# A Fourier filter ahead of a mixture of experts: dense transform replaced by a two-stage transform of 48 by 52 points

## Chip, cores, metric

One core of one Trainium2 chip. The metric is the device time of one execution in microseconds (us), the median of repeated runs.

## The reference

Each of 8 sequences of 2496 tokens and 256 channels is filtered along the tokens in the Fourier domain. Each token then goes to the best of 8 experts.

```python
X = np.fft.rfft(x, axis=1)                       # x: (8, 2496, 256) f32
F = (filt_r + 1j * filt_i)[None, :, :]           # (1249, 256)
y = np.fft.irfft(X * F, n=x.shape[1], axis=1)
# ... x = y.reshape(19968, 256)
logits = x @ w_gate + modality_bias[modality_id]
e_idx = np.argmax(logits, axis=1)                # top 1
# ... per expert e, on its tokens:
h = np.maximum(x[mask] @ w1[e], 0.0)
out[mask] = gate_w[mask, None] * (h @ w2[e])
```

## The kernel before

The filter is a dense transform: cosine and sine tables of 2496 by 1249 are generated on the chip, forward and inverse are plain matmuls in 16 bit. The output goes to DRAM as `xm_d`. Everything behind it (gating, sort, scatter, experts, gather) reads `xm_d` and is not changed. (The name `BF16` in the code stands for float16.)

```python
for cg in range(n_cg):                     # 4 groups of 512 columns (2 sequences)
    # ... x[b, s0:s0+sw, :] loaded in 128 KB pieces, cast to f16 on VectorE
    for kt in range(n_kt):
        ps_r = fpp.tile([P, CG], F32, tag="psr")
        ps_i = fpp.tile([P, CG], F32, tag="psi")
        for st in range(n_st):
            nc.tensor.matmul(ps_r[:kw, :], lhsT=fcos[:sw, st, k0:k0 + kw], rhs=xr[:sw, st, :], ...)
            nc.tensor.matmul(ps_i[:kw, :], lhsT=fmsin[:sw, st, k0:k0 + kw], rhs=xr[:sw, st, :], ...)
        # ... four products with the filter on VectorE, sum and difference on GpSimd
        # ... stored to Yr_d, Yi_d
# ... inverse tables generated
for cg in range(n_cg):
    # ... Yr_d, Yi_d loaded
    for nt in range(n_st):
        ps = ipp.tile([P, CG], F32, tag="ips")
        for kt in range(n_kt):
            nc.tensor.matmul(ps[:nw, :], lhsT=icos[:kw, kt, n0:n0 + nw], rhs=yrs[:kw, kt, :], ...)
            nc.tensor.matmul(ps[:nw, :], lhsT=imsin[:kw, kt, n0:n0 + nw], rhs=yis[:kw, kt, :], ...)
        # ... copied on ScalarE, stored to xm_d
# ...
xTc = gwp.tile([P, N], BF16, name=f"xTall{dc}")
nc.sync.dma_start_transpose(xTc, xm_d[:, dc * P:(dc + 1) * P])   # first reader of all of xm_d
```

## Time and profile before

| | us |
|---|---|
| median of 3 runs | 2477.0 |
| span of the profiled run | 2468.9 |
| filter (until the first transposing read of `xm_d`) | 1063.6 |
| all the rest | 1405.3 |

The first transposing read of `xm_d` cannot begin before the last store of the filter has landed, and nothing of the rest can begin before it. So its start splits the time in two, in both kernels. I call it the filter's end. The lines are in the prediction.

### The profile page before, as it was taken

The page shows a single profiled execution, that of the slowest core. Times are in us where ns is not written, and L with a number is a line of the kernel's source. Part 1 is how long each engine was busy: PE and PEld are TensorE (multiplying, and loading weights), DVE is VectorE, ACT ScalarE, POOL GpSimd, SP SyncE. Part 2 cuts the span into 40 slices and gives each one's busy share as a digit, 9 for nine tenths or more (in the row PEclk, how much of TensorE's full clock was granted, in tenths as well). Part 3 has the DMA queues.
Part 4 walks back from the last instruction along what each step waited for, and adds up shares of the span by engine and source line. Part 5 has one row for each costly group of instructions (what it writes and reads, how often), then busy time and mean ns, then how long its engine had stood idle before and what let it go on. Part 6 is the DMA issues. An engine that isn't in the chain of part 4 may idle for free. (4 is left out here: it accounts for less than half of the span.)

```text
span 2468.9 us, 22991 instructions
## 1 busy us (share of the span) xinstructions
PE 1283.3 (52%) x7228; PEld 617.4 (25%) x7228; DVE 634.8 (26%) x1325; ACT 443.8 (18%) x775; POOL 445.6 (18%) x487
## 2 busy tenths in 40 slices
PE   2469786876339999912000000000899999991000
PEld 0014232322114444402000000000555555550000
DVE  6873233323770000007100000000233333332122
ACT  4320000000341111101000000000455555550000
POOL 0012222221000000000013333345000000006665
PEclk9999898978669999965555555555999999996555
DMA  2112222211101221190971111117222222224466
GB/s 73 37 49 66 64 61 64 63 45 63 41 6 39 69 71 29 32 172 4 37 230 53 52 53 53 51 43 224 77 75 76 76 72 76 76 67 145 138 185 204
DMA packets 319271, 192.16 MB, mean 78 GB/s; under 512 B 172580, under 2 KB 306678, under 8 KB 319158
## 3 DMA queue, kind: packets, MB, share of 16 engines
q1 hardware_dynamic: 306678, 160.01, 25.8%
q0 software_dynamic: 12480, 30.69, 4.4%
q8 instruction: 65, 1.06, 0.2%
q14 instruction: 48, 0.39, 0.1%
HBM read 80.93 MB, written 87.38 MB: 68 GB/s over the span
## 5 line engine op out<-in xcount | busy, mean ns | idle before, releaser
L487 PE MATMUL hps<-w1sb,xT 128*128 x736 | 249.1, 380 | 555.5 <-DMA xT<-xs_d 555.5
L498 DVE COPY hT_sb<-hTps 128x512 f16<-128x512 f16 x368 | 156.3, 425 | 885.5 <-PE hTps L497 885.5
L182 PE MATMUL ps_i<-xr,fmsin 128*128 128x512 f16 (+2 forms) x800 | 325.9, 420 | 89.3 <-ACT fmsin L121 88.6
L238 PE MATMUL ps<-yrs,icos 128*128 128x512 f16 (+2 forms) x800 | 315.7, 395 | 103.6 <-ACT icos L125 83.3
L180 PE MATMUL ps_r<-xr,fcos 128*128 128x512 f16 (+2 forms) x800 | 324.2, 418 | 81.4 <-DVE xr L170 64.4
L491 ACT ACTIVATE h_sb<-hps 128x512 f16<-128x512 f32 x368 | 220.8, 600 | 625.8 <-PE hps L487 610.1
L240 PE MATMUL ps<-yis,imsin 128*128 128x512 f16 (+2 forms) x800 | 314.3, 393 | 0.0
L517 POOL DMA_INDIRECT ot<-os_d,pos_i32c x156 | 148.2, 950 | 572.2 <-DVE pos_i32c L514 502.9
L501 PE MATMUL ops<-w2sb,hT_sb 128*128 x1472 | 240.3, 272 | 0.3 <-DVE hT_sb L498 0.2
L487 PEld LDWEIGHTS <-xT 128*128 128x128 f16 x736 | 64.2, 98 | 570.5 <-issue 557.5
L449 POOL DMA_INDIRECT xs_d<-xg,pos_i x156 | 148.8, 954 | 267.8 <-DMA xs_d<-xg,pos_i 238.2
L501 PEld LDWEIGHTS <-hT_sb 128*128 128x128 f16 x1472 | 134.9, 97 | 67.6 <-DVE hT_sb L498 46.1
L182 PEld LDWEIGHTS <-fmsin 128*128 128x128 f16 (+2 forms) x800 | 83.2, 106 | 271.2 <-ACT fmsin L121 105.8
L497 PE MATMUL hTps<-ident,h_sb 128*128 128x128 f16 x1472 | 144.1, 220 | 13.1 <-ACT h_sb L491 0.5
L202 POOL TENSOR_TENSOR yr<-t,t 128x512 f16<-128x512 f32 (+1 forms) x40 | 50.9, 1272 | 487.6 <-DVE t L199 268.6
L238 PEld LDWEIGHTS <-icos 128*128 128x128 f16 (+2 forms) x800 | 80.8, 101 | 211.9 <-ACT icos L125 109.0
L497 PEld LDWEIGHTS <-h_sb 128*128 128x128 f16 x1472 | 97.4, 97 | 131.8 <-ACT h_sb L491 103.8
L180 PEld LDWEIGHTS <-fcos 128*128 128x128 f16 (+2 forms) x800 | 83.0, 106 | 155.1 <-issue 46.8
L121 ACT ACTIVATE imsin<-fr,zbias 128x1280 f16<-128x1280 f32 (+3 forms) x20 | 26.7, 1335 | 502.6 <-DMA yis<-Yi_d 442.9
L170 DVE CAST xr<-tmp 128x256 f16<-128x256 f32 (+1 forms) x160 | 50.1, 313 | 232.7 <-DMA tmp<-in_x_dram 232.7
L240 PEld LDWEIGHTS <-imsin 128*128 128x128 f16 (+2 forms) x800 | 81.1, 101 | 99.1 <-issue 12.2
L506 ACT COPY osb<-ops 128x256 f32<-128x256 f32 x184 | 68.4, 372 | 206.9 <-PE ops L501 205.1
(108 smaller groups left out, 737.5 us busy)
## 6 DMA issues: line engine op xcount, KB each, us to landing
os_d<-osb SPq DMA_DIRECT2D x184, 128.0 KB
out_dram<-ot SPq DMA_DIRECT2D x156, 128.0 KB
tmp<-in_x_dram SPq DMA_DIRECT2D x152, 128.0 KB
xs_d<-zz SPq DMA_DIRECT2D x23, 512.0 KB
xg<-xm_d SPq DMA_DIRECT2D x156, 64.0 KB
xm_d<-yo SPq DMA_DIRECT2D x152, 64.0 KB
tmp<-in_moe_w_dram SPq DMA_DIRECT2D x16, 512.0 KB
tmp<-in_moe_w_dram SPq DMA_DIRECT2D x64, 128.0 KB
```

The lines of the kernel that those rows point to most:

```text
L180: nc.tensor.matmul(ps_r[:kw, :], lhsT=fcos[:sw, st, k0:k0 + kw], rhs=xr[:sw, st, :], start=(st == 0), stop=(st == n_st - 1))
L182: nc.tensor.matmul(ps_i[:kw, :], lhsT=fmsin[:sw, st, k0:k0 + kw], rhs=xr[:sw, st, :], start=(st == 0), stop=(st == n_st - 1))
L238: nc.tensor.matmul(ps[:nw, :], lhsT=icos[:kw, kt, n0:n0 + nw], rhs=yrs[:kw, kt, :], start=(kt == 0), stop=False)
L240: nc.tensor.matmul(ps[:nw, :], lhsT=imsin[:kw, kt, n0:n0 + nw], rhs=yis[:kw, kt, :], start=False, stop=(kt == n_kt - 1))
L449: nc.gpsimd.indirect_dma_start(out=xs_d[:, :], out_offset=IOA(ap=pos_i32[:, t:t + 1], axis=0), in_=xg[:, :], in_offset=None)
L487: nc.tensor.matmul(hps, lhsT=xTs[dc][:, nsl], rhs=w1sb[:, ds(ej, 1), dc, fc * 512:(fc + 1) * 512], start=(dc == 0), stop=(dc == n_dc - 1))
L491: nc.scalar.activation(h_sb[:, fc * 512:(fc + 1) * 512], hps, AF.Relu)
L497: nc.tensor.transpose(hTps[:, k, :], h_sb[:, ft * P:(ft + 1) * P], ident)
L498: nc.vector.tensor_copy(hT_sb[:, fg * 4:(fg + 1) * 4, :], hTps)
L501: nc.tensor.matmul(ops, lhsT=hT_sb[:, ft, :], rhs=w2sb[:, ds(ej, 1), ft, :], start=(ft == 0), stop=(ft == n_ft - 1))
L506: nc.scalar.copy(osb, ops)
L517: nc.gpsimd.indirect_dma_start(out=ot[:, :], out_offset=None, in_=os_d[:, :], in_offset=IOA(ap=pos_i32c[:, t:t + 1], axis=0))
```

## The change

The intent: 2496 = 48 x 52, so the transform can be done as 48-point transforms (stage 1), twiddles and 52-point transforms (stage 2), the product with the filter, 52-point inverse (still stage 2), and 48-point inverse (stage 3). This takes 496 matmuls of 512 columns where there were 3200. The matrices are small and made on the chip. Between the stages, rows and columns swap through DRAM (`b1_d`, `b2_d`). The experts are untouched. The diff, cut to the new stages:

```diff
-    # dense tables, forward and inverse loops (see above)
+    N1, N2 = 48, 52                       # NS = 24, NTT = 26, KA = 96, KB = 104
+    # ... w1m, wbm (96 x 96), w2m, a1m, a2m (24 matrices of 104 x 104) made from iota and Sin
+    gen = tc.alloc_tile_pool(name="gen", bufs=1)          # their scratch
+    # ...
+    for src, dst in ((w2m, a1m), (w2x, a2m)):
+        for s0 in range(0, NS, SPB):
+            # ... 8 transposes on TensorE into tp
+            nc.vector.tensor_copy(
+                dst[:, s0:s0 + SPB, :].rearrange("p s (jr t) -> p s t jr", jr=4),
+                tp[:, :, :KB].rearrange("p s (t jr) -> p s t jr", jr=4))
+    gen.release()
+    # ... filter loads, 18 DMAs on GpSimd (f32 to f16)
+    with tc.tile_pool(name="fx", bufs=3) as xp, tc.tile_pool(name="fr", bufs=3) as rp, \
+         tc.tile_pool(name="fbig", bufs=2) as bp, tc.tile_pool(name="fpsum", bufs=4, space=PSUM) as pp:
+        def stage1(g):
+            # ... x of two half groups: nc.gpsimd.dma_start(xt[:, bi, :, :], xb[:, t0:t1, :])
+            for t in range(0, NTT, EV):                    # EV = 2: 1024 columns
+                # ... 2 matmuls with w1m into ps
+                t1_sb = rp.tile([KA, EV, CG], BF16, tag="t1")
+                nc.scalar.copy(t1_sb, ps[:KA])             # every sixth on VectorE
+                nc.sync.dma_start(b1_d[g, t:t + EV].rearrange("t p c -> p t c"), t1_sb)
+        def stage2(g):
+            for hh in range(NH):                           # 2 halves of 6 pairs
+                # ... t2: 4 loads from b1_d on SyncE
+                for s in range(0, sn, EV):
+                    # ... 2 forward matmuls: ps <- w2m, t2
+                    nc.scalar.copy(xf, ps[:KB])
+                    nc.vector.tensor_mul(p1, xf, g1[...])
+                    nc.vector.tensor_mul(p2, xf, g2[...])
+                    pz = pp.tile([P, EV, CG], F32, tag="ps")
+                    # ... 4 inverse matmuls: pz <- a1m, p1 and a2m, p2
+                    nc.scalar.copy(z, pz[:KB])
+                    nc.sync.dma_start(b2_d[g, ...], z)
+        def stage3(g):
+            for hh in range(NH):
+                # ... t4: 4 loads from b2_d on SyncE
+                for t in range(0, tn, EV):
+                    # ... 2 matmuls with wbm into ps
+                    nc.vector.tensor_scalar_mul(yo[...], ps[...], 1.0 / S)
+                for bi in range(BPG):
+                    nc.sync.dma_start(xm_d[...], yo[:, bi, :, :])
+        for g in range(NG + 2):                            # NG = 4
+            if g < NG: stage1(g)
+            if 0 < g <= NG: stage2(g - 1)
+            if g > 1: stage3(g - 2)
```

## The prediction

> **What bounds the kernel now.** I read the busy digits first, then a table of stretches cut where the work changes, then the groups by shape. The program is a chain of stages, and no engine bounds all of it, so each stage has to be read by itself.
>
> ```profile
> PE   2469786876339999912000000000899999991000
> PEclk9999898978669999965555555555999999996555
> DMA  2112222211101221190971111117222222224466
> ```
>
> The filter fills slices 1 to 17; the rest is gating, sorting, scatter, experts and gather. The stretches:
>
> ```profile
> core 0: us, PE busy (x) PEld busy (x) DVE busy (x) ACT busy (x) POOL busy (x), PEclk, DMA share, GB/s
> 0.00:597.00 597.00, 417.93 (x1600) 161.84 (x1600) 254.16 (x431) 63.95 (x62) 104.33 (x90) 0.93 0.19 56
> 597.00:736.00 139.00, 43.69 (x113) 14.71 (x114) 104.72 (x98) 51.36 (x39) 0.00 (x0) 0.61 0.12 38
> 736.00:1064.00 328.00, 324.52 (x1491) 146.06 (x1488) 4.32 (x8) 48.38 (x81) 0.14 (x1) 0.99 0.16 48
> 1064.00:1113.00 49.00, 0.93 (x29) 0.88 (x30) 3.16 (x3) 0.25 (x2) 0.00 (x0) 0.50 1.30 212
> 1113.00:1178.00 65.00, 13.30 (x321) 12.30 (x317) 45.93 (x215) 9.48 (x40) 1.23 (x2) 0.50 0.00 1
> 1178.00:1271.00 93.00, 0.59 (x2) 0.50 (x2) 8.72 (x46) 0.00 (x0) 2.57 (x3) 0.50 1.33 159
> 1271.00:1663.00 392.00, 0.00 (x0) 0.00 (x0) 0.00 (x0) 0.00 (x0) 149.35 (x157) 0.50 0.17 51
> 1663.00:1722.00 59.00, 0.00 (x0) 0.00 (x0) 0.00 (x0) 0.00 (x0) 35.05 (x69) 0.50 0.73 229
> ...
> 2229.00:2469.00 240.00, 1.44 (x12) 0.83 (x12) 57.95 (x158) 0.37 (x1) 148.23 (x156) 0.51 0.57 172
> ```
>
> Three rows are the filter: forward transform (597 us, 1600 matmuls, PE 70% busy, stalls while cosine tables are generated and x arrives in 128 KB pieces), inverse tables (139 us, DVE 75% busy), inverse transform (328 us, PE 99% busy). So 1064 us of 2469 are PE and table work for a dense 2496-point transform. From 1064 on, everything waits for the complete filtered tensor: two transposing DMA reads start at 1063.6 us. The remaining 2468.9 - 1063.6 = 1405 us are untouched by the change, and they cannot start early in either version. The 8.1 us between the span and the median of 2477.0 I carry over too.
>
> The durations that I need for the new stages:
>
> ```profile
> L238 PE MATMUL ps<-yrs,icos 128*128 128x512 f16 x684 | 270.0, 395 | 95.0 <-ACT icos L125 74.7 <-DMA yis<-Yi_d 20.4
> L506 ACT COPY osb<-ops 128x256 f32<-128x256 f32 x184 | 68.4, 372 | 206.9 <-PE ops L501 205.1 <-issue 1.8
> L243 ACT CAST yo<-ps 128x512 f16<-128x512 f32 x76 | 44.2, 585 | 261.2 <-PE ps L240 248.7 <-DMA xm_d<-yo 12.5
> L198 DVE TENSOR_TENSOR t<-ps_r,Gr_sb 128x512 f32<-128x512 f32 x36 | 24.9, 692 | 57.7 <-PE ps_r L180 55.3 <-POOL yr L202 2.3
> L498 DVE COPY hT_sb<-hTps 128x512 f16<-128x512 f16 x368 | 156.3, 425 | 885.5 <-PE hTps L497 885.5
> ```
>
> Matmuls of 512 columns start 0.216 us apart at full clock (about 463 in each of the two 100 us windows from 800 to 1000). ACT needs 585 ns for 512 columns and 372 for 256, which is 0.83 ns a column: 1.01 us for 1024. DVE needs 692 ns for 512 f32 columns out of PSUM, about 0.53 us of columns and 0.15 fixed: 1.22 us for 1024. A 16-bit source goes at twice that rate (425 ns for 512).
>
> **What the Trainium skill says.** "VectorE: DVE Perf Modes", section "The perf-mode tier table (the rule you actually need)", gives a two-input elementwise op on 16-bit SBUF data 2x, and f32 PSUM sources 1x. The trace agrees on PSUM; it has no 16-bit two-input op, so 1024/2/0.96 + 150 = 0.69 us for the new filter product is an estimate from that page and the fixed part above. "DMA: Bandwidth & Descriptors", "SWDGE vs HWDGE vs iDMA", says that a DMA which changes the type must be issued from GpSimd; that is why the new x and filter loads are there, and no run here shows what such a cast moves per second. The same page, "Why a DMA increments its semaphore by 16 and not by 1", lets a transfer use the largest count up to 16 that divides its outer sizes: 13 engines for the new loads of 26 rows, 12 for those of 24; no run here shows it yet. "TensorE: Matmul & The Clock Gate", "Part 1: The HAM clock gate (the "warmup" mystery)", has the clock halve when PE idles: the trace agrees with 0.61 in the table stretch and 0.50 in the DMA stages.
>
> **The change, part by part.** Removed: all three filter rows, 1064 us (3200 matmuls, 107 us of ACT sines, the DVE table work, 160 x loads). Added: 48 small transposes of constants and 496 matmuls of 512 columns (104 + 288 + 104), 107 us at 0.216. Eviction replaces PE as the heavy work. ACT gets 44 + 96 copies of 1024 columns, 140 x 1.01 = 141 us. DVE gets 8 copies x 1.22, 96 products x 0.69, 48 evictions x 1.22 and 8 of half that size x 0.69: 10 + 66 + 59 + 6 = 141 us. DMA gets x 20.4 MB, four passes over intermediates of 10.2 MB, the output 10.2 and filters 5: 76 MB. At the 420 GB/s that the 4 KB rows of the zero fill reached (1242 to 1268 us) that is 181 us, at the 300 of 1 KB rows (172 GB/s at a share of 0.57 in the last row of the stretches) 253.
>
> No one engine therefore needs more than 141 us, and if all overlapped, the filter would take 260 us. I expect it not to. The built program's order on each engine shows stages strung one behind another: PE runs stage 1 of groups 0 and 1, stage 2 of group 0, stage 1 of group 2, stage 2 of group 1, stage 3 of group 0, stage 1 of group 3, and so on, and DVE the same. Within it, on the path:
> - Start: constants on DVE and POOL's 18 filter loads, about 38 us (f32 ops as in the old table code, 0.8 to 2.8 us each; x buffers reuse that scratch, so x waits for it). Then four half groups of x, 5.1 MB f32 per group, at the 229 GB/s of the weight stretch: 45 us, 2 us to land, 7 last copies at 1.35 us: 94 us.
> - Stage 1 copies have three buffers; each is held for 1.0 us of copy, 0.4 of issue and about 2.3 until landed, so 1.25 to 1.35 us a copy, 15 us for a group instead of 11. Twice exposed (groups 2 and 3): 30 us.
> - Stage 2: PE's order puts the next pair's forward matmuls behind the product of this pair. The cycle is copy 1.01, product 0.69, three matmuls and drain 0.86, semaphores 0.3: 2.85 us a pair, where ACT's own need is 2.02. Twelve pairs and the drain make 38 us. For groups 0 and 3 the second half's fourth load is queued behind the last stores, 4 and 2 us. 4 x 38 + 6 = 158 us.
> - Stage 3: 14 evictions, 16 us, and twice about 4 us because the last load of each half is issued behind stores that are not ready: 24 us, four times 96. The next stage's loads wait behind its store once, 4.5 us, and the last output store takes 5.
>
> Sum: 94 + 30 + 158 + 96 + 4.5 + 5 = 388 us for the filter. In the rest, the modality ids (8-byte pieces) now are issued after the two transposing reads instead of before: about 5 us later. 388 + 1405 + 5 + 8 = 1806 us.
>
> **The rivals.** Full overlap: the scheduler's order lets ACT and DVE work beside each other, and the filter takes 260 to 300 us. For it: 141 us each, buffers of three and four. Against: the engine orders above. It makes 1680 to 1720. DMA as the bound: casting loads might move far less than 229 GB/s, or the 12- and 13-engine loads crowd the low engines. At 100 GB/s x alone takes 204 us, of which only the first two groups lie in front of everything, and the filter becomes about 450 us: 1870; at 60 GB/s, about 1970. For it: nothing in the trace casts in DMA. Against: the rows are 13 KB, and large rows moved at 420. Cold PE: matmuls at half clock, 0.43 us. In stage 2 this adds 0.65 us a pair, 31 us over 48, to 1837. For it: PE is used 45% there; against: the first 100 us of before ran 31% busy with the clock at 1.00.
>
> **Range and chances.** The removed time is measured, and the untouched 1405 us repeat to a few us; all doubt is in the 388. Individual terms are good to 15%, and the x loads are the worst known, with a tail to the slow side. I give 1735 to 1890, a filter of 317 to 472 us. For the change not to gain 2%, the filter would have to take over 1010 us, four times its DMA time at 300 GB/s: faster 0.98, same 0.01, slower 0.01.
>
> **What would show it.** In the profile after: the transposing reads start near 388 us, and the gap from there to the end is 1405 to 1412 us. ACT's 1024-column copies mean about 1.01 us, the DVE product about 0.69 (1.2 would mean that the 2x rate was not taken, and cost some 25 us), the PSUM evictions 1.22. The stage 2 pairs repeat every 2.8 us or so with PE's forward matmul waiting for the product. ACT and DVE each stay under 45% busy over the filter, and DMA under 70%. Stage 1 of group 0 begins near 50 us. The prediction is wrong if DMA share stays near 1 in the filter (the casts bound it), if ACT is near 90% busy there (full overlap), or if the stages after 1064 us change length.

## The result, and the profile after

| | before | after | predicted |
|---|---|---|---|
| median of 4 runs, us | 2476.9 | 1895.4 (1889.1 to 1898.5) | 1806 (1735 to 1890) |
| filter's end in the trace | 1063.6 | 484.4 | 388 |
| rest of the span | 1405.3 | 1411.8 | about 1410 |

The ratio after to before is 0.765 (0.763 to 0.767). Ratios here are the mean time of one kernel's runs over that of the other's of the same rounds, so not quite the ratio of the medians quoted. The gain is large, but 89 us smaller than predicted, and the result lies 5 us outside the range. The whole miss is in the filter (+96 us); the rest was right to 2 us, and the span and the median differ by 1 us where I had carried over 8.

The busy digits of the page after, 40 slices of 47 us:

```profile
PE   1346656453020000000000004999999999900000
DVE  8012333334065000000000001333333333321222
PEclk9555555555555555555555556999999999955555
DMA  6855454434944981111111073222223222255566
```

The filter is now slices 1 to 10. In the first of them DVE reads 8 (it makes the constants). From the second on no engine is near 9 and the clock reads 5; DMA reads 8 in the second and is near half after it. In stretches, with the columns as in the prediction:

```profile
core 0: us, PE busy (x) PEld busy (x) DVE busy (x) ACT busy (x) POOL busy (x), PEclk, DMA share, GB/s
0.00:115.00 115.00, 29.40 (x102) 14.12 (x103) 42.81 (x81) 25.64 (x26) 23.83 (x46) 0.72 0.76 158
115.00:484.00 369.00, 198.10 (x443) 84.53 (x441) 126.70 (x156) 117.90 (x118) 1.01 (x3) 0.52 0.44 124
484.00:540.00 56.00, 9.54 (x314) 9.12 (x314) 5.09 (x9) 8.42 (x40) 0.12 (x1) 0.50 1.15 186
```

From 115 to 484 us ACT and DVE are busy a third of the time, PE half, DMA 44%. So neither an engine nor the transfer rate bounds this stretch: waits do. (The start is another matter: DVE is 89% busy up to 34 us, and from there to 115 us the DMA share is 0.86.) The groups of instructions within the filter show that each single cost but that of the last line came out as expected, and name the waits (busy us and mean ns of one, then idle us before them and what ended it):

```profile
L302 ACT CAST xf<-ps 104x1024 f16<-104x1024 f32 x48 | 48.6, 1013 | 106.7 <-PE ps L299 99.7 <-issue 6.9
L306 DVE TENSOR_TENSOR p<-xf,g 104x1024 f16<-104x1024 f16 x48 | 33.2, 692 | 129.5 <-ACT xf L302 129.5
L333 DVE TENSOR_SCALAR yo<-ps 96x1024 f16<-96x1024 f32 (+1 forms) x56 | 59.8, 1135 | 76.4 <-PE ps L331 76.4
L331 PE MATMUL ps<-t,wbm 96*96 96x512 f16 x104 | 44.5, 615 | 77.9 <-DMA t<-b_d 66.2 <-issue 11.6
L237 DVE COPY a1m<-tp 104x832 f16<-104x832 f16 x3 | 11.2, 3969 | 0.0
```

The copy takes 1.01 us and the product 0.69, as predicted; the 76.4 us before `yo` are stage 3's wait for its loads (8 half groups); the constants' evictions, 4 us each (three more, of `a2m`, took as long), are a surprise. Two timelines show where it goes. One pair of stage 2, from the trace after (start, length, engine, line; in brackets the idle time before):

```profile
122.96 0.69 DVE L306 TENSOR_TENSOR p<-xf,g 104x1024 f16<-104x1024 f16 x1 [1.97 <-ACT xf L302]
...
123.71 0.59 PE L310 MATMUL pz<-p,a1m 104*104 104x512 f16 x1 [0.55 <-DVE p L306]
...
124.09 1.06 PE L299 MATMUL ps<-t,w2m 104*104 104x512 f16 x2
...
125.23 1.01 ACT L302 CAST xf<-ps 104x1024 f16<-104x1024 f32 x1 [1.02 <-PE ps L299]
...
126.28 0.69 DVE L306 TENSOR_TENSOR p<-xf,g 104x1024 f16<-104x1024 f16 x1 [2.02 <-ACT xf L302]
```

This is the circle that sets the pace: product, inverse matmul `a1m` (it waits for the product), then behind it in PE's order the next pair's forward matmuls, their copy, the next product. It goes round in 126.28 - 122.96 = 3.32 us: 0.75 from product to matmul, 0.38 and 0.43 between matmul starts, 0.71 to the copy, 1.05 from copy to product. 3.31 is the median over all four groups.

And stage 3 of the trace after, SyncE's DMA issues, VectorE's evictions and PE's matmuls around the end of one half:

```profile
424.12 0.81 SPq L338 DMA_DIRECT2D xm_d<-yo  x2
424.97 5.40 SPq L323 DMA_DIRECT2D t<-b_d  x4
```

```profile
420.02 4.07 DVE L333 TENSOR_SCALAR yo<-ps 96x1024 f16<-96x1024 f32 x4
434.58 2.35 DVE L333 TENSOR_SCALAR yo<-ps 96x1024 f16<-96x1024 f32 x2 [10.49 <-PE ps L331]
```

```profile
433.48 2.77 PE L331 MATMUL ps<-t,wbm 96*96 96x512 f16 x6 [12.21 <-DMA t<-b_d]
```

The last eviction of a half ends at 424.1, only then do its two stores go out, and only behind them four loads. These are the 24th to 27th of the 32 loads of stage 3, four to a half: the first of them is the last load of the next half, the other three belong to the half after that. The one that the next half waits for takes 1.6 us to issue, where most take 0.7. The first matmul that needs it starts at 433.5, 8.5 us after its issue began, and the next eviction begins 10.5 us after the last. In the first half of group 0, where no output store stands ahead, the same way from the issue of the last load (229.5 us) to the first matmul (233.8) took 4.4 us.

### The profile page after: what moved, and what is told of

It reads as the page before. It is cut to its first block, busy times and chain, and to the rows that moved or that the text cites. A ratio compares the mean times of both kernels' runs of the same rounds, so it can differ in the third digit from the quotient of the medians.

```text
span 1896.2 us, 16727 instructions
## 1 busy us (share of the span) xinstructions
PE 725.2 (38%) x4572; PEld 393.9 (21%) x4572; DVE 442.9 (23%) x1031; ACT 423.6 (22%) x737; POOL 370.3 (20%) x445
## 3 DMA queue, kind: packets, MB, share of 16 engines
q1 hardware_dynamic: 262146, 157.41, 34.2%
## 5 line engine op out<-in xcount | busy, mean ns | idle before, releaser
L621 DVE TENSOR_SCALAR ot<-ot,gate_sb 128x256 f32<-128x256 f32 x156 | 58.1, 380 | 168.3 <-DMA out_dram<-ot 71.1
L333 DVE TENSOR_SCALAR yo<-ps 96x1024 f16<-96x1024 f32 (+1 forms) x56 | 59.8, 1135 | 76.4 <-PE ps L331 76.4
L310 PE MATMUL pz<-p,a1m 104*104 104x512 f16 x96 | 58.6, 610 | 41.2 <-DVE p L306 41.2
L331 PE MATMUL ps<-t,wbm 96*96 96x512 f16 x104 | 44.5, 615 | 77.9 <-DMA t<-b_d 66.2
L302 ACT CAST xf<-ps 104x1024 f16<-104x1024 f32 x48 | 48.6, 1013 | 106.7 <-PE ps L299 99.7
L285 ACT CAST t_sb<-ps 96x1024 f16<-96x1024 f32 x44 | 42.7, 1010 | 125.5 <-DMA b_d<-t_sb 67.8
L279 PE MATMUL ps<-xt,w1m 96*96 96x512 f16 x104 | 45.6, 585 | 61.6 <-ACT t_sb L285 48.2
L299 PE MATMUL ps<-t,w2m 104*104 104x512 f16 x96 | 50.8, 632 | 36.7 <-DMA t<-b_d 19.6
L306 DVE TENSOR_TENSOR p<-xf,g 104x1024 f16<-104x1024 f16 x48 | 33.2, 692 | 129.5 <-ACT xf L302 129.5
L312 PE MATMUL pz<-p,a2m 104*104 104x512 f16 x96 | 60.4, 629 | 0.1
```

The source lines that it names most:

```text
L310: nc.tensor.matmul(pz[:KB, i, :], lhsT=a1m[:, s0 + s + i, :], rhs=p1[:, i].rearrange("p b d -> p (b d)"), start=True, stop=False)
L312: nc.tensor.matmul(pz[:KB, i, :], lhsT=a2m[:, s0 + s + i, :], rhs=p2[:, i].rearrange("p b d -> p (b d)"), start=False, stop=True)
L333: nc.vector.tensor_scalar_mul(yo[:, :, t:t + ev, :].rearrange("p b t d -> p t b d"), ps[:KA, 0:ev, :].rearrange("p t (b d) -> p t b d", b= ...
L621: nc.vector.tensor_scalar_mul(ot2, ot, gate_sb[:, t:t + 1])
```

## The experiments

Theory: three terms make the miss. (A) PE at half clock, inside a circle that the order of PE's instructions closes. (B) Loads that stand in SyncE's queue behind stores which are not ready. (C) A slow start. The rival to A is that the clock is a symptom and only order or DMA counts; the rival to B is that the transfers take that long anyway.

Chips differ: before took 2474 to 2478 us on the chips of c1, e5 to e7 and e8 to e11, and 2445 to 2448 on those of e1 to e4 and f1 to f3. The traces put this into the part behind the filter (1404 to 1412 us against 1374 to 1384). So I compare the filter's end in the trace, 484.4 in the changed kernel, and the ratio to before on the same chip. All had three rounds. The changed kernel itself was not run on the second sort of chip; but e1, e2, f1 and f2, which leave the start as it is, began stage 2 there at 112.7 to 115.2 us, against 115.4 and 115.7 in the two runs of the changed kernel, so up to there the chips differ by 3 us at most in these runs. No run compares them over the rest of the filter.

**c1, control.** No edit.

> The changed kernel unaltered, as a control on the same chip as the three runs beside it: the kernel before took 28 us less on the chip of the last four runs than on the first, so ratios and the filter's end are compared, not times. Expected: filter end within 2 us of 484, ratio 0.765 or a little lower if the chip makes the remainder shorter.

Measured: filter's end 485.4, ratio 0.764. As expected. One thing stood out: its page has the clock at 9 for the first three slices where the first run had 9, 5, 5. More on that below.

**e1, spare matmuls** fill PE's wait in stage 2.

```diff
                     pz = pp.tile([P, EV, CG], F32, tag="ps")
+                    for f in range(2):
+                        nc.tensor.matmul(pz[:KB, f % EV, :], lhsT=w2m[:, s0 + s, :], rhs=t2[:, s, :],
+                                         start=True, stop=True)
```

> Two spare matmuls (w2m on t2) are written into each pz tile before the real ones, which overwrite them; the result stays right. They give PE work while it waits for copy and product; the built order also lets the next pair's forward matmuls go ahead of this pair's product. Theory A (half clock costs the miss in stage 2): the granted clock in 120 to 450 us rises from 0.50-0.53 to over 0.8, matmuls start 0.22 us apart, a stage 2 pair takes about 2.85 us instead of 3.31, and the filter's end moves from 484 to about 462 us (48 x 0.46 = 22 us). Theory B (waits for DMA and for copy and product, clock is only a symptom): clock may rise, but the filter ends within 6 us of 484. If the clock stays at 0.50, PE has 8 x 0.425 = 3.4 us a pair and the filter ends some 5 us later.

Measured: clock 0.64 to 0.78 in stretches of 50 us (0.81 to 0.86 within stage 2 alone), pair 1.9 to 2.3 us (medians by group), filter's end 433.8 (-51), ratio 0.741. The gain is over twice what A allowed (a pair of 2.85), so more than the clock had changed: the spare matmuls also let the next pair's forward matmuls ahead of `a1m`. e5 and e8 take the two apart.

**e5, order alone.**

```diff
+                nxt = fwd(0)                      # fwd(s): the two forward matmuls of pair s
                 for s in range(0, sn, EV):
-                    # ... forward matmuls of pair s into ps
+                    ps = nxt
+                    if s + EV < sn:
+                        nxt = fwd(s + EV)
```

> Only the order: the next pair's forward matmuls are emitted before this pair's product ones, no spare matmuls. The spare matmuls of the earlier run changed the order too, and its pair went from 3.31 to about 2.0 us with the clock at 0.76. If the order made the gain, the pair falls here to 2.1-2.6 us (PE's own 6 x 0.425 = 2.55) with the clock near 0.50, filter end 445 to 460. If the clock made it, the pair stays at 3.0 to 3.3 us, filter end over 475.

Measured: filter's end 439.2 (-45), ratio 0.746, pairs of 1.8 to 2.4 us by group. The clock did not stay at 0.50. The stretches, first of the changed kernel, then of this run:

```profile
100.00:150.00 50.00, 23.25 (x51) 9.63 (x50) 11.57 (x17) 18.67 (x19) 1.00 (x2) 0.50 0.49 127
```

```profile
100.00:150.00 50.00, 26.37 (x79) 12.62 (x80) 16.38 (x25) 25.01 (x27) 1.01 (x2) 0.68 0.53 140
```

79 matmuls instead of 51 in the same 50 us, and the recorded clock up from 0.50 to 0.68. Order opens the circle, PE then pauses less, and the clock rises by itself. The spare matmuls need not be there.

**e8, the clock alone** (relative error 0.82). Its output is wrong, which doesn't matter for the time.

```diff
-                        nc.tensor.matmul(ps[:KB, i, :], lhsT=w2m[...], rhs=t2[:, s + i, :], ...)
+                        nc.tensor.matmul(ps[:KB, i, 0:CG // 2], lhsT=w2m[...], rhs=t2[:, s + i, 0:CG // 2], ...)
                         # the four inverse matmuls likewise
-                    nc.scalar.copy(xf..., ps[:KB])
+                    nc.scalar.copy(xf, ps[:KB, :, None, 0:CG // 2].to_broadcast([KB, EV, BPG, D]))
                     # z likewise
```

> Wrong result on purpose: the six matmuls of a stage 2 pair compute 256 columns instead of 512, and the two copies read these columns twice, so that copies, products, stores and (but for a few places) the order stay as they were. A matmul at half clock then starts 0.21 us after the last, as one of 512 columns would at full clock. It prices the clock alone, with the order of the changed kernel: the cycle copy 1.05, product to matmul 0.74, three matmuls 0.6 to 0.65, drain about 0.4 gives 2.8 us instead of 3.31, and 48 x 0.5 = 24 us, filter end about 461. If the order alone were the cause and the clock none: under 8 us, pair 3.1 or more.

Measured: pair 2.67 us in all four groups, filter's end 452.7 (-32), ratio 0.752, recorded clock still 0.50 to 0.60. With the changed kernel's order, matmul time at half clock therefore costs 0.64 us a pair. A holds, and so does the part of its rival that names the order: order and clock are two keys to one circle. Their gains do not add: 45 (e5) and 32 here, but 51 in e1, which has the order and most of the clock.

**e2, output stores from GpSimd.**

```diff
-                    nc.sync.dma_start(
+                    nc.gpsimd.dma_start(
                         xm_d[b * S:(b + 1) * S, :]...
```

> The filter's output stores go out from GpSimd instead of SyncE, so that the loads of stages 2 and 3 no longer queue behind stores that are not ready. Theory B (queueing behind the stores makes the 8.5 to 10.5 us waits of stage 3): the wait of the 1024-column evictions for PE falls from about 10 to 4 us a half, and the filter ends 20 to 45 us earlier than 484. Rival (the loads need that long anyway, or start late because their source was stored late): under 8 us.

Measured: filter's end 424.9 (-59), ratio 0.738; the best of the single edits. The 14 evictions of a group take 15 us from first to last instead of 25, with one wait ahead. The issues and evictions at the same place as above, in this run:

```profile
389.61 10.64 SPq L323 DMA_DIRECT2D t<-b_d  x8
```

```profile
385.21 14.86 DVE L333 TENSOR_SCALAR yo<-ps 96x1024 f16<-96x1024 f32 x14 [9.29 <-PE ps L331]
```

The loads of the next halves go out while this half is still being evicted, and 14 evictions run without a gap. Of what the edit gained, 4 x 10 us are these waits, the rest lies around the last group: its stage 2 no longer waits 10 us for loads behind a store, and its stage 3 follows the one before 1 us after it instead of 10.

**f1 and f2, queue or path?** e2 changed two things: who waits in which queue, and the path by which the stores are issued. f1 puts the stores into ScalarE's queue, f2 the stage 3 loads, with the stores left on SyncE.

```diff
-                    nc.sync.dma_start(xm_d[...]...        # f1
+                    nc.scalar.dma_start(xm_d[...]...
-                    nc.sync.dma_start(t4[jr:KA:4, :, :]... # f2
+                    nc.scalar.dma_start(t4[jr:KA:4, :, :]...
```

> Output stores from ScalarE's queue. If the place behind the stores is the cause, stage 3 runs its 14 evictions in about 15 us per group as with GpSimd (25 in the changed kernel), and the filter ends at 425 to 445, some us later than with GpSimd because ScalarE waits for the last eviction before its next copies. If GpSimd's path made the gain, stage 3 stays at 23 to 25 us and the filter ends after 470.

> Stage 3 loads from ScalarE's queue, stores left on SyncE. The loads no longer stand behind output stores, but stand among ScalarE's copies and wait there for the z stores. If the place in the queue is the cause, stage 3 goes at 15 to 18 us a group and the filter ends at 425 to 455; if not, after 475. The stage 2 loads of the last group still queue behind output stores, so less than with the stores moved.

Measured: filter's end 431.8 and 431.7 (-53), ratio 0.740 in both, evictions 15 us (f1, but 18 in the last group) and 16 us (f2) a group. Three ways of taking loads and stores out of one queue give nearly the same, so it is the place in the queue and not the path. B is shown. What stays open is how much of the 8.5 us above is due to the two stores' own transfer, 1.25 MB just ahead of the load: no run separates that from the late issue.

**e3, six buffers for the store sources.**

```diff
-                t1_sb = rp.tile([KA, EV, CG], BF16, tag="t1")
+                t1_sb = rp.tile([KA, EV, CG], BF16, tag="t1", bufs=6)
                 # z likewise
```

> Six buffers instead of three for the copies of stage 1 and for z, so that a store may take twice as long before a copy waits. Theory B: the copies' wait for the b1 stores (67.8 + 58.1 us in the groups) mostly goes; stage 1 of groups 2 and 3 fall from 20 to about 13 us each, and the start from 115 to about 105: the filter ends 20 to 25 us earlier. Rival (the queue is limited by how fast SyncE issues or how fast the transfers go): under 8 us.

Measured: filter's end 477.1 (-7), ratio 0.757. Stage 1 did get shorter (group 2 from 29 to 20 us between its first and last copy, group 3 from 26 to 14) and stage 2 of group 0 began at 107.0 instead of 115.4. Most was given back: stage 2 of group 1 began 14 us earlier but took 45.0 instead of 39.5 us, and the last group's began only 7 us earlier. So the store wait is real but was mostly not on the path: a miss of this expectation.

**e4, x first.**

```diff
+    xp = tc.alloc_tile_pool(name="fx", bufs=3)
+    early = {(0, 0): load_x(0, 0), (0, 1): load_x(0, 1), (1, 0): load_x(1, 0)}
     gen = tc.alloc_tile_pool(name="gen", bufs=1)
```

> The x buffers are taken before the scratch of the constants and the first three half groups of x are issued at the very start instead of at 34 us and later. Theory C (the start is bound by when x arrives): stage 2 of group 0 begins 25 to 45 us before 115, and the whole time falls by as much. Rival (the start is bound by the making of constants and by the 1.2 us copy-store cycle of 26 copies): first copy a few us earlier, stage 2 under 12 us earlier.

Measured: x issued from 1.7 us on instead of 34, yet the first copy of stage 1 still came at 44.4 and stage 2 began at 109.4 (-6); filter's end 479.4 (-5), ratio 0.759. The rival held: the first copy did not wait for x.

**e9, the constants' evictions** walk the output in order.

```diff
-                    dst[...].rearrange("p s (jr t) -> p s t jr", jr=4),
-                    tp[:, :, :KB].rearrange("p s (t jr) -> p s t jr", jr=4))
+                    dst[...].rearrange("p s (jr t) -> p s jr t", jr=4),
+                    tp[:, :, :KB].rearrange("p s (t jr) -> p s jr t", jr=4))
```

> The six reordering evictions of the constants (4.0 us each) walk their output in order and their PSUM source with a stride, instead of the other way about. If the strided 16-bit write is what costs, they fall to 1 to 1.5 us each, x is issued some 10 us earlier than 34, the first copy of stage 1 comes at about 28 to 32 us instead of 44, and the filter ends 10 to 16 us earlier. If the stride costs as much on the reading side, nothing moves.

Measured, the line that answers to L237 above:

```profile
L237 DVE COPY a1m<-tp x3: 1021/1025/1025, 18.0 to 19.9; 104x832 f16<-104x832 f16 x3
```

1.02 us instead of about 4.0 (minimum, median and maximum in ns). x was issued at 23.4 instead of 34.2, the first copy came at 34.0 instead of 44.1, the filter ended at 472.7 (-12), ratio 0.760. PE runs the 48 transposes ahead of stage 1, and they wait for these evictions: that was what the first copy waited for.

**e6, e7, f3, e10, e11: together.** No new edits. e6 is e1 + e2 + e3 + e4; e7 is e6 without spare matmuls; f3 is e5 + e2; e10 is e5 + e2 + e3 + e4 + e9; e11 is e10 with spare matmuls.

> All four edits together: spare matmuls, output stores from GpSimd, six buffers for the store sources, x issued first. If the gains add: 51 + 59 + 7 + 5 = 122 us, filter end 362. If the small gains of buffers and early x were masked by the waits that the others take away, the filter ends at 310 to 345. If the two large ones overlap, over 385.

> The same without the spare matmuls. If the clock and the DMA queue are separate terms, this ends 45 to 55 us later than the run with all four, with a pair at 3.31 us and the clock at 0.50-0.55; if the freed queue makes the rest dense enough to lift the clock by itself, within 25 us of it and the clock over 0.6.

> Order of the forward matmuls and output stores from GpSimd, nothing else. Independent terms: 46 + 59 = 105 us, filter end 375 to 385. If they share a part (stage 2 of the last group lies beside stage 3 in either), 385 to 400.

> Forward matmuls first (order), output stores from GpSimd, six buffers, x first, evictions in output order; no spare matmuls. With the four-edit run at 375, the order in place of spare matmuls should hold the pair near 2.0 to 2.2 us, and the evictions give what they give alone: filter end 355 to 370, ratio about 0.713 to 0.720.

> The same with the two spare matmuls a pair as well. If the order leaves ACT (2.02 us a pair) as the limit, a warmer clock is worth little: within 8 us of the run without them. If the half clock still costs in the stages, 15 us or more earlier.

| run | filter's end | ratio | time on its chip, us | pair of stage 2, us (median within groups) |
|---|---|---|---|---|
| e6 | 375.4 | 0.721 | 1784.0 | 2.11 |
| e7 | 408.6 | 0.734 | 1815.7 | 3.31 |
| f3 | 381.0 | 0.721 | 1761.0 | 2.02 |
| e10 | 356.5 | 0.7135 | 1768.3 | 1.81 |
| e11 | 352.9 | 0.712 | 1764.0 | 1.81 |

e6 fell between what adding the gains (362) and overlap (over 385) would give, and e7 is 33 us behind it, neither 45 to 55 nor under 25: I did not foresee that spare matmuls are worth less once the rest is dense, and no run shows why. f3 came out as for independent terms: order and queue are separate. e10 and e11 came out as expected but for the pair of e10 (2.0 to 2.2), and the spare matmuls are worth 3.6 us there. ACT's two copies of a pair take 2.02 us, so a median of 1.81 only says that the steps are uneven: the mean within a half is 2.03 us in e10. e10 beats both kernels: 0.7135 against 0.764 for the changed kernel's control, with correct results.

## Why the prediction was wrong

The mechanism was right: what was removed, the string of stages, no bound engine, the untouched rest. The filter was mis-sized, and the sum can be settled in the trace after. The rows are cut at the first copy of a stage 2 and at the end of the last eviction of a stage 3, so where stages overlap, as stage 1 of group 3 does with both its neighbours, a cut divides them:

| stretch | predicted | measured | |
|---|---|---|---|
| start, to the first copy of stage 2 | 94 | 115.4 | +21.4 |
| stage 2 of group 0, stage 1 of group 2 | 42 + 15 | 70.3 | +13.3 |
| stage 2 of group 1, stage 3 of group 0 | 38 + 24 | 74.2 | +12.2 |
| stage 1 of group 3 | 15 | 17.4 | +2.4 |
| stage 2 of group 2, stage 3 of group 1 | 38 + 24 | 76.7 | +14.7 |
| loads of the last stage 2 behind the stores | 4.5 | 10.1 | +5.6 |
| stage 2 of group 3, stage 3 of group 2 | 40 + 24 | 78.0 | +14.0 |
| stage 3 of group 3 | 24 | 34.3 | +10.3 |
| last store | 5 | 8.0 | +3.0 |

By term, the +96 are: stage 3's waits 44 (the largest), stage 2's pairs 22, the start 21, the loads of the last stage 2 6, and the last store 3.

- **Stage 2, "three matmuls and drain 0.86" in a cycle of 2.85 us.** This step failed: the cost of a matmul was wrong. I took matmuls at full clock, 0.216 us; they started 0.43 us apart, and the pair took 3.31: 48 x 0.46 = 22 us. It is the rival "cold PE", which I had written down at +31 us and not believed. e8 prices the clock at 0.64 us a pair, 31 us, just that rival's figure, since my cycle was 0.18 too long otherwise.
- **Why the rival was dismissed.** My argument was that the first 100 us of before ran with the clock at 1.00. That was a misreading. The trace of before has no clock record ahead of 166 us (the control c1 has none ahead of 168), and the view shows 1.00 until the first one. The matmuls of that very stretch say otherwise (first the group of before in 50 to 100 us, then its timeline):

```profile
L180 PE MATMUL ps_r<-xr,fcos 128*128 128x512 f16 x23 | 11.3, 624 | 7.0 <-ACT fcos L125 7.0
```

```profile
61.71 1.46 PE L182 MATMUL ps_i<-xr,fmsin 128*128 128x512 f16 x3 [3.23 <-ACT fmsin L121]
```

  Three matmuls of 512 columns take 1.46 us, that is two steps of 0.42 and a tail of 0.62: half clock, at 31% busy. The evidence against the rival was evidence for it, and it lay in the trace before. In c1, where the stretch from 100 to 150 us also reads 1.00, the pair takes 3.31 us and matmuls start 0.43 apart as everywhere.
- **Stage 3, "twice about 4 us because the last load of each half is issued behind stores that are not ready".** Right cause, wrong size. The trace gives 76.4 us in 8 waits, 9.6 each, where I had 8 x 4 = 32. It was one load that stood behind the stores, as predicted; but 4 us is about what a load took with no output store ahead of it (4.4 us from issue to matmul). Behind the stores the wait was 10.5 us: 0.85 for the stores' issue, 8.5 from there to the matmul, 1.1 to the eviction. In the first halves of groups 0 to 2 it was stores of `z` that stood ahead, and the waits were 8.5 to 9.2 us. e2, f1 and f2 show the cause for the waits behind output stores; the wait ahead of a group stayed (9.3 us in e2, above). The "4.5 us" for the next stage's loads was 10.1 for the same reason.
- **Start, "Then four half groups of x ... at the 229 GB/s of the weight stretch: 45 us".** The miss is not in the constants, for which I had 38 us: x was issued at 34.2. This was luck. Six of their evictions took 4.0 us each, which I had not foreseen; without that (e9) x went out at 23.4, so the rest of the 38 was too long. From the issue of x to the first copy of stage 2 I had 56 us; the trace after has 81.2 and e9, 11 us earlier, 81.0. In this stretch the DMA share is 0.86 at 193 GB/s, and it carries more than the four half groups: by 102 us 14 of the 16 loads of x, seven half groups, had been issued. ACT's stage 1 copies waited 46 us in it for earlier stores to land. Six buffers begin stage 2 at 107.0 and early x at 109.4 instead of 115.4, both together (e7) at 99.9. That the transfers of x and the stores hold each other up is likely, but no run shows it: the cause of this part stays open.
- **Stage 1, "1.25 to 1.35 us a copy".** The copies took longer (26 and 29 us between the first and the last of a group), but e3 shows that little of it was on the path.
- **Right:** copy 1.01, product 0.69 (which agrees with the 2x for 16-bit operands in the Trainium skill, "VectorE: DVE Perf Modes", section "The perf-mode tier table (the rule you actually need)") and eviction 1.22 us; ACT and DVE under 45% and DMA under 70% busy; the casts not the bound; stage 1 near 50 us (44.1); rest 1411.8 against 1410.

All three large terms came out longer than predicted, so their errors did not cancel, and a range of 15% a term was too narrow.

## What to carry to other kernels

Read the clock from the spacing of matmuls of equal size, not from the clock digit alone, and look for a closed circle through the order of PE's instructions: emitting the next forward matmuls ahead of the product took a third off each pair and let the clock rise by itself. Keep loads that the next stage needs and stores that wait for this stage in different issuing queues; it was worth 53 to 59 us here, whichever engine took them. When a store's source gets more buffers, ask first whether its wait is on the path.

## What the Trainium skill lacked or had wrong

- "DMA: Bandwidth & Descriptors", section "Issuing engines are not separate DMA queues", says that issuing from several engines "will only save the time on the sequencer it takes to initiate the DMA, which is usually small relative to the DMA itself". That section does not name the in-order wait: a load behind a store whose source is not ready waits with it. Moving 16 stores or 32 loads to another issuing engine took 53 to 59 us off (e2, f1, f2).
- "TensorE: Matmul & The Clock Gate", "Part 1: The HAM clock gate (the "warmup" mystery)", has the clock rise after about 3.4 us of sustained activity and fall after an idle window as long, but gives no figure for how much pause inside such a window is too much. Here PE started six matmuls per 3.31 us, about 0.43 us apart with one step of 1.22, and stayed at half clock through stage 2 of all four groups; with shorter pauses (e5) the recorded clock was 0.61 to 0.74 within stage 2, and many steps were 0.21 to 0.22.
- The same part warns under "Seeing it yourself" that clock events in a trace can be unreliable. The runs add one case: before the first event there is no record, and the view reads 1.00 while matmuls start 0.43 us apart (before until 166 us, c1 until 168 us).
- "Vector Engine (DVE) Microarchitecture Reference", section "5.2 Measured stream behaviour on trn2 (trn3 not measured)", gives 2.5 ns a column for 4-byte data written at a step of 24 words; that section has no figure for 16-bit data. Here 832 columns of 16 bit written at a step of 26 elements took 4.0 us (4.8 ns a column); read from PSUM at a step of 4 elements and written in order, 1.02 us (e9).
